# The first half of a threshold attention: four of its slots get their weights turned by TensorE instead of by VectorE and DMA

## The chip, the cores and the metric

The kernel runs on one core of a Trainium2 chip, as one program. The metric is the device time of one launch in microseconds; the kernel before takes 865.78 us, the median of three runs (862.09 to 871.87). Five engines work side by side, each through its own list of instructions in order: TensorE (PE, matrix products), VectorE (DVE), ScalarE (ACT), GpSimd (POOL), and SyncE (SP), which here only issues transfers. A PE product writes to PSUM, a small memory of its own that DVE and ACT read. Transfers are carried out by 16 DMA engines which all queues share. An engine waits at an instruction until the others have signalled that its inputs are ready and its output buffer is free.

## The reference

Two blocks follow one another. First an attention in which only the keys whose score lies within `tau` of the row's largest keep a weight; 8 batches, 8 heads, 576 positions, 64 values a head, all float32:

```
scores = (q @ k.T) / 8
thresh = max(scores, row) - tau
scores = where(scores >= thresh, scores, -1e9)
attn   = exp(scores - max);  attn /= sum(attn) + 1e-9
x      = (attn @ v), heads side by side      # 4608 tokens x 512
h      = x @ w_in                            # 1024 wide
solu   = h * softmax(h)
ln     = (solu - mean) / sqrt(var + 1e-6) * g_ln
out    = ln @ w_out                          # 4608 x 512
```

`w_in` and `w_out` come in as 64-bit floats, and the kernel makes 32-bit ones of them itself.

## The kernel before

**Slots and rounds.** Heads go in pairs. A slot is 128 query rows of the two heads of a pair against all 576 keys; 18 slots make a batch, 144 the whole. Slots 0 to 7 are the first 256 positions of the four pairs of batch 0, two slots to a pair. The main loop goes in rounds, `rnd`; round n does for slot n: the scores (`scores`, L472), the row maxes (`maxes`, L494, DVE), the threshold (`ramp`, L509, ACT, one for each head) and the exponentials with their sums (`exps`, L518, ACT). For slot n-1 it does the division by the sums (`normalise`, L525 to L528, POOL) and `blocks`: DVE transposes the weights in squares of 32 (L540), and after the second slot of a pair three DMAs (L549, L551) move the squares into place, so that keys lie on the partitions (`wT<-T`). Three or four rounds after a pair's second slot the product with v (`attend_steps`, L582, tile `pv`) runs on PE, and ACT copies it (L614) into `xh`, the tokens for the second block.

**The second block, in quarters.** Tokens go in tiles of 128. A tile takes four PE steps, at most one a round: two for h (`ff_h`, L647, against `w_in`) and two for the output (`ff_o`, L752, against `w_out`). Between them lie max, exponential, product, statistics, two normalised copies (`ff_max` L662, `ff_exp` L671, `ff_mul` L677, `ff_stats` L692 and POOL's L696 to L703, `ff_norm` L713, `ff_norm2` L718), four DMAs (`V<-u`, L729) and a transpose (`ff_turn`, L739, tile `uT`). The first two tiles of h need slots 0 to 7, and all of `w_in`; with the kernel before their four quarters stand in rounds 11 to 14.

**The weights.** They come in 16 pieces of 512 KB, one a round: `weight_load` (L270) four rounds ahead, `weight_a` (L284, L287 on DVE, L290 on ACT), `weight_b` (L302, DVE), `weight_c` (L312, POOL), and for `w_out` `weight_gain` (L317, ACT) and a pair of DMAs that lay down a copy with its halves swapped (`w<-w`, L324). The first o step is therefore in round 17 at the soonest.

**Order.** All is issued in the order in which the Python code runs, one list for each engine. What stands around the change: `load_at` says in which round q, k and v of later pairs are loaded (SP's list); `preps` says when those are turned (by `turn`, L337); `pv_due` when a product with v is due; `ready` from which round a tile's h may start; `late`, `middle` and `begin` hold jobs for later rounds. PSUM has two tiles for scores (`s0`, `s1`) and two for all else (`p0`, `p1`, lent by `take` and given back to `pairs_free`).

Of the kernel before, what the change touches and what calls it, by code (L numbers as in the profile page):

```python
# [8 lines left out]
F32 = mybir.dt.float32  # L9
# [7 lines left out]
P = 128  # L17
# [3 lines left out]
def kernel(  # L21
# [47 lines left out]
    ident = const.tile([P, P], F32, name="ident")  # L69
    swapped = const.tile([P, 64], F32, name="swapped")  # L70
    w1 = const.tile([P, NP, DFF], F32, name="w1")
# [24 lines left out]
    xh = {}  # L96
# [5 lines left out]
    def take(name):  # L102
        tag = pairs_free.pop(0)
        return tag, ps_mm.tile([P, 1024], F32, tag=tag, name=name)
# [114 lines left out]
    def constants():  # L219

        nc.gpsimd.memset(seed, 0.0)
        nc.scalar.activation(out=ntau, in_=seed, func=AF.Exp)
        make_identity(nc, ident)
        for g in range(2):
            of = 64 + 32 * (1 - g)
            nc.gpsimd.tensor_copy(
                out=swapped[ROWS[1], 32 * g : 32 * g + 32], in_=ident[ROWS[1], of : of + 32]
            )
        nc.gpsimd.memset(mhalf, -0.5)
        nc.gpsimd.memset(mone, -1.0)  # L230
        nc.gpsimd.memset(zero, 0.0)

        nc.vector.tensor_scalar(
            out=scl, in0=tau_t, scalar1=0.0, scalar2=SCALE, op0=ALU.is_ge, op1=ALU.mult
        )
        nc.vector.tensor_scalar(
            out=tau_t, in0=tau_t, scalar1=0.0, scalar2=104.0, op0=ALU.max, op1=ALU.min
        )  # L240
        nc.vector.tensor_scalar(out=ntau, in0=tau_t, scalar1=-1.0, scalar2=None, op0=ALU.mult)
# [89 lines left out]
    def turn(spare, x, lhsT_of, swap=False):  # L331

        o = spare["base"] + 64 * x
        to = slice(o, o + 64)
        for r in range(2):
            for y in range(2):
                nc.tensor.matmul(  # L337
                    out=spare[r][ROWS[y], to], lhsT=lhsT_of(r, y),
                    rhs=swapped[ROWS[1]] if swap and r else ident[ROWS[r], ROWS[r]],
                    start=True, stop=True,  # L340
                )
# [106 lines left out]
    live = {}  # L448

    def scores(s, items):  # L450
        b, kind, hp, r = slots[s]
# [55 lines left out]
    def ramp(s, x):  # L507
        d = live[s]
        nc.scalar.activation(  # L509
            out=d["w"][x], in_=d["w"][x] if d["loose"] else d["ps"][x][:, 0:S], func=AF.Prelu, bias=d["nth"][x], scale=-1.0,  # L510
            alpha=1.0e30,
        )
# [9 lines left out]
    def normalise(s):  # L522
        d = live[s]
        sm = d["sm"]
        nc.gpsimd.tensor_scalar(out=sm, in0=sm, scalar1=1e-9, scalar2=None, op0=ALU.add)  # L525
        nc.gpsimd.tensor_tensor(out=sm, in0=sm, in1=mone, op=ALU.pow)  # L526
        for x, w in enumerate(d["w"]):
            nc.gpsimd.tensor_scalar(  # L528
                out=w, in0=w, scalar1=sm[:, x : x + 1], scalar2=1.0, op0=ALU.mult, op1=ALU.mult
            )  # L530
# [27 lines left out]


    def attend_steps(key):  # L560
        b, kind, hp = key
        unit = units[key]
        wT = unit["wT"]
        unit["y"] = take("pv")
        _, y = unit["y"]
        y = y.rearrange("p (u n) -> p u n", u=2)

        for e in range(2) if kind == 2 else [None]:
            for m in range(NK):
                for u in range(2):  # L570
                    d, h0 = source(b * NP + (hp if e is None else e + 2 * u))
                    for h in range(2):
                        if e is None:
                            how = "p (r g x) -> p g r x" if b < 2 else "p (g r x) -> p g r x"
                            to = y[ROWS[h], u, 0:P].rearrange(how, r=2, g=2)
                            rhs = wT[ROWS[u], :, m, :, h]
                        else:
                            to = y[ROWS[h], u, 64 * e : 64 * e + 64].rearrange(
                                "p (g x) -> p g x", g=2
                            )  # L580
                            rhs = wT[ROWS[u], :, m, e, h]
# [9 lines left out]
                        yield  # L591

    def attended(key):
        b, kind, hp = key
        tag, y = units.pop(key)["y"]
        y = y.rearrange("p (u n) -> p u n", u=2)[:, :, 0:P]
# [10 lines left out]
        else:  # L607
            if hp == 0:
                xh[b, kind] = work.tile(
                    [P, NP, 256], F32, tag=f"xh{(2 * b + kind) % 4}", bufs=1, name="xh"  # L610
                )
            how = "p (r u y) -> p u r y" if b < 2 else "p (u g x r) -> p u g r x"
# [185 lines left out]
    for s, (b, kind, hp, r) in enumerate(slots):  # L798
        if r == 1:
            pv_due.append((s + LAG_PV + (s < 6 or s in (11, PER - 1, PER + 9)), (b, kind, hp)))  # L800
# [17 lines left out]
    for at, job, hf, what in (  # L818
        (11, load_one, 0, "q"),
        (10, load_one, 0, "k"),  # L820
        (15, load_one, 1, "k"),
        (16, load_one, 1, "q"),
        (17, load_v, 0, (0,)),
        (18, load_v, 0, (1, 2)),
        (PER + 6, load_v, 1, (0,)),
        (PER + 7, load_v, 1, (1, 2)),
    ):
        load_at.setdefault(at, []).append(lambda job=job, hf=hf, what=what: job(1, hf, what))
# [31 lines left out]
    with tc.manual_schedule():  # L860
# [16 lines left out]
        whole = {0: 1, 2: 2, 4: 3}  # L877
        for r, hf, parts in ((0, 0, (0,)), (1, 0, (1, 2)), (3, 1, (0,)), (5, 1, (1, 2))):
            load_at[r] = [lambda hf=hf, parts=parts: load_v(0, hf, parts)]

# [9 lines left out]
        while True:  # L890
# [10 lines left out]
            if rnd == NS:  # L901
# [8 lines left out]
                assert quarter != 3  # L910
            if rnd == 13:
                prev, cur, quarter = cur, None, 0
# [9 lines left out]
            if more:  # L922
# [18 lines left out]
                maxes(rnd, loose)  # L941
                ramp(rnd, 0)
                if rnd == 0:
                    weight_a(0)
                if not loose:
                    keeps(rnd, 0)
                    keeps(rnd, 1)
                ramp(rnd, 1)
                exps(rnd)
            if rnd in whole:  # L950
# [30 lines left out]
            elif step == ("h", 1):  # L981
                ff_h(cur, 1, None, beside)
                quarter = 2
                by = rnd + 2 * (rnd == 14)
                late.setdefault(by, []).append(lambda t=cur: (ff_max(t), ff_exp(t)))
# [9 lines left out]
                if cur == (0, 1, 1):  # L995
                    middle.setdefault(rnd + 6, []).append(lambda t=cur, at=rnd + 6: ff_turn(t, at))
                else:
                    late.setdefault(at, []).append(lambda t=cur, at=at: ff_turn(t, at))
                if not more:
# [15 lines left out]
            if attending is not None:  # L1015
# [6 lines left out]
                elif kind < 2 and hp == NP - 1:  # L1022
                    ready.append((rnd + 1, [(b, kind, 0), (b, kind, 1)]))
            if rnd - 1 in live:
                blocks(rnd - 1)
# [8 lines left out]
            if rnd == 3:  # L1034
                gains()
            if rnd in pieces:
                x = pieces[rnd]
                weight_b(x)
                for y in {0: (3, 4), 11: (), 12: (15,)}.get(x, (x + 4,)):
                    if y < len(pieces):  # L1040
                        weight_load(y)
                if x + 1 < len(pieces):
                    weight_a(x + 1)
            for job in load_at.pop(rnd, []):
# [39 lines left out]
```

## Time and profile before

| | |
|---|---|
| median of three runs | 865.78 us |
| the profiled execution | 864.95 us, of which 863.2 are from the first to the last instruction (the span) |
| TensorE busy | 817.0 us (95%) |
| VectorE, ScalarE, GpSimd busy | 673.5, 572.1, 495.1 us |
| granted TensorE clock, mean | 0.981 of full speed |
| DMA moved | 168.54 MB, 195 GB/s |
| scores of round 6, 9, 11, 13 begin | 39.07, 50.89, 68.22, 79.53 us |
| scores of round 17, 19, 20 begin | 102.52, 116.31, 120.75 us |

The busy share is the time in which an engine has any instruction running; products on PE overlap, so a busy PE is not one at its peak. A wait belongs to the engine that stands idle, and names the one whose signal ended it. The chain that ended last is followed backwards from the last instruction; a line in it is time that the end depended on. A float32 product appears in the trace as two records, each with a weight load of its own (`PEld`). `64*64` is the part of PE's 128 x 128 array that a record uses: four products in different quarters run at the same time.

### The profile page before, as it was taken

To read this page: it belongs to the slowest core of one execution; us is meant where nothing else is said; L and a number is where in the kernel's file an instruction comes from. 1 tells how busy PE (TensorE), PEld (TensorE's weight loads), DVE (VectorE), ACT (ScalarE), POOL (GpSimd) and SP (SyncE) were. 2 spreads that over 40 slices of the span, in tenths; PEclk is the share of its full clock that TensorE was granted. 3 is DMA by queue.
4 is the path that set the end of the run, shared out by engine and by line. 5 is a ranking of instruction groups with operands and counts; after the bars stand their busy time and mean duration, and the time that the engine had idled before them with its cause. 6 is when DMAs were issued, how large, how long until landed. Compare 5 with 4: busy or idle time off the path is not lost.

```text
span 863.2 us, 36114 instructions
## 1 busy us (share of the span) xinstructions
PE 817.0 (95%) x15361; PEld 634.7 (74%) x15361; DVE 673.5 (78%) x1232; ACT 572.1 (66%) x1153; POOL 495.1 (57%) x936
## 2 busy tenths in 40 slices
PE   4659789999999999999999999999999999999997
PEld 3437567777688888888788886777788888887655
DVE  4987777978788888888788887888888888787361
ACT  5876867777667767777677766767677776775121
POOL 2876756566666656565656655565666655555120
PEclk9878999999999999999999999999999999999999
DMA  9999796997878778888788787888788887555312
GB/s 288 243 254 251 185 203 162 234 248 196 224 196 219 202 196 208 220 214 198 201 202 222 198 194 192 212 222 206 183 228 229 193 196 186 154 141 140 69 38 62
DMA packets 83712, 168.54 MB, mean 195 GB/s; under 512 B 15448, under 2 KB 45152, under 8 KB 83552
## 3 DMA queue, kind: packets, MB, share of 16 engines
q1 hardware_dynamic: 82416, 164.25, 75.5%
q8 instruction: 120, 1.97, 1.0%
q10 hardware_dynamic: 1136, 2.00, 0.7%
q14 instruction: 40, 0.33, 0.1%
HBM read 46.14 MB, written 9.44 MB: 64 GB/s over the span
## 4 chain that ended last, share of the span: by engine, by line
PE 84%; DMA 6%; ACT 4%; issue 2%; DVE 2%; POOL 1%; SPq 1%; ACTq 0%; DVEq 0%
PE o_ps L752 26%; PE h_ps L647 23%; PE s_ps L472 16%; PE pv L582 15%; DMA wT<-T 4%; PE h_ps L637 3%; ACT w L509 1%; ACT w L518 1%; DMA qT<-flip 1%; DMA w<-w 1%; DVE w L494 1%; DMA k<-in_k_dram 1%; ACT qT L374 0%; PE s_ps L337 0%; POOL w L528 0%
## 5 line engine op out<-in xcount | busy, mean ns | idle before, releaser
L752 PE MATMUL o_ps<-w,uT 64*64 64x256 f32 x4608 | 273.1, 376 | 4.3 <-issue 1.9
L494 DVE CUSTOM_DVE_ANT_0 w<-s_ps,tau_t 128x576 f32<-128x576 f32 x280 | 200.0, 751 | 94.4 <-PE s_ps L472 67.0
L509 ACT ACTIVATE w<-s_ps,nth 128x576 f32<-128x576 f32 x280 | 197.0, 739 | 110.8 <-DVE nth L494 90.8
L752 PEld LDWEIGHTS o_ps<-w,uT 64*64 64x64 f32 x4608 | 221.5, 133 | 59.3 <-ACT xh L614 12.0
L528 POOL TENSOR_SCALAR w<-w,sm 128x576 f32<-128x576 f32 x288 | 221.5, 781 | 14.3
L540 DVE STREAM_TRANSPOSE T<-w 128x576 f32<-128x576 f32 x288 | 207.5, 755 | 22.0 <-POOL w L528 20.6
L647 PE MATMUL h_ps<-w,xh 64*64 64x512 f32 x1856 | 223.1, 589 | 0.7 <-issue 0.7
L518 ACT ACTIVATE w<-w,ntau 128x576 f32<-128x576 f32 x288 | 219.8, 768 | 0.0
L582 PEld LDWEIGHTS pv<-wT,v 64*64 64x64 f32 x5760 | 179.7, 137 | 37.4 <-issue 12.8
L472 PE MATMUL s_ps<-kT,qT 64*64 64x512 f32 (+1 forms) x2048 | 177.1, 413 | 14.0 <-ACT w L509 12.0
L582 PE MATMUL pv<-wT,v 64*64 64x128 f32 (+1 forms) x5760 | 179.5, 266 | 9.7 <-DMA wT<-T 7.2
L647 PEld LDWEIGHTS h_ps<-w,xh 64*64 64x64 f32 x1856 | 131.7, 133 | 65.4 <-issue 10.6
L525 POOL TENSOR_SCALAR sm<-sm 128x2 f32<-128x2 f32 x144 | 34.7, 241 | 203.7 <-ACT w L518 200.1
L526 POOL TENSOR_TENSOR sm<-sm,mone 128x2 f32<-128x2 f32 x144 | 105.8, 735 | 12.0
L472 PEld LDWEIGHTS s_ps<-kT,qT 64*64 64x64 f32 x2048 | 76.0, 136 | 21.1 <-ACT w L509 16.4
L614 ACT COPY xh<-pv 128x256 f32<-128x256 f32 x64 | 25.0, 390 | 83.3 <-PE pv L582 83.2
L713 ACT ACTIVATE V<-u,nb,rs 128x1024 f32<-128x1024 f32 x36 | 44.7, 1241 | 39.6 <-POOL nb L703 32.6
L739 DVE STREAM_TRANSPOSE uT<-V 128x1024 f32<-128x1024 f32 x36 | 44.3, 1230 | 15.2 <-DMA V<-u 14.8
L518 ACT ACTIVATION_READ_ACCUMULATOR w<-w,ntau 128x1 f32 x288 | 55.9, 194 | 0.0
L677 DVE TENSOR_TENSOR u<-h_ps,u 128x1024 f32<-128x1024 f32 x36 | 42.8, 1189 | 9.7 <-ACT u L671 9.7
L718 DVE TENSOR_SCALAR u<-u,rs,nb 128x1024 f32<-128x1024 f32 x36 | 35.5, 987 | 17.2 <-ACT V L713 17.1
L662 DVE TENSOR_REDUCE hm<-h_ps 128x1 f32<-128x1024 f32 x36 | 43.0, 1193 | 6.0 <-PE h_ps L647 3.3
(88 smaller groups left out, 562.9 us busy)
## 6 DMA issues: line engine op xcount, KB each, us to landing
wT<-T SPq DMA_DIRECT2D x160, 288.0 KB, 6.2
wT<-T SPq DMA_DIRECT2D x64, 576.0 KB, 5.5
V<-u SPq DMA_DIRECT2D x144, 64.0 KB, 3.4
out_dram<-ob SPq DMA_DIRECT2D x71, 128.0 KB, 2.5
q<-in_q_dram SPq DMA_DIRECT2D x24, 288.0 KB, 6.1
qT<-flip SPq DMA_DIRECT2D x48, 144.0 KB, 3.8
k<-in_k_dram SPq DMA_DIRECT2D x24, 288.0 KB, 5.9
kT<-flip SPq DMA_DIRECT2D x48, 144.0 KB, 4.2
```

The source lines that it names most:

```text
L472: nc.tensor.matmul(out=ps[h][ROWS[y], ks], lhsT=lhsT, rhs=d["kT"][ROWS[h], ks], start=True, stop=True,)
L494: nc.vector.tensor_tensor_reduce(out=w, in0=ps[:, 0:S], in1=(zero if loose else tau_t).to_broadcast([P, S]), scale=1.0, scalar=BIG, op0=AL ...
L509: nc.scalar.activation(out=d["w"][x], in_=d["w"][x] if d["loose"] else d["ps"][x][:, 0:S], func=AF.Prelu, bias=d["nth"][x], scale=-1.0, al ...
L518: nc.scalar.activation(out=w, in_=w, func=AF.Exp, bias=ntau, scale=1.0, accum_out=sm[:, x : x + 1])
L526: nc.gpsimd.tensor_tensor(out=sm, in0=sm, in1=mone, op=ALU.pow)
L528: nc.gpsimd.tensor_scalar(out=w, in0=w, scalar1=sm[:, x : x + 1], scalar2=1.0, op0=ALU.mult, op1=ALU.mult)
L540: nc.vector.transpose(out=T[:, :, r, h, :], in_=w)
L582: nc.tensor.matmul(out=to, lhsT=d["v"][ROWS[u], (h0 + h - u) % 4 if b > 1 else h0 + h, m ^ 4 * u if m < 8 and b < 2 else m,], rhs=rhs, sta ...
L647: mm = nc.tensor.matmul(out=h[ROWS[y], f], lhsT=x[ROWS[r], c, ROWS[y]], rhs=w1_parts[ROWS[r], c, part ^ r], start=part == 0 and c == 0, st ...
L713: nc.scalar.activation(out=V, in_=u, func=AF.Identity, bias=nb, scale=rs)
L739: nc.vector.transpose(out=uT, in_=d["V"].rearrange("p y (m x) -> p m y x", x=32))
L752: nc.tensor.matmul(out=d["o"][ROWS[z], 512 * (r ^ other) : 512 * (r ^ other) + 256], lhsT=d["uT"][ROWS[r], m].rearrange("p y x -> p (y x)" ...
```

## The change

For slots 4 to 7 (`EARLY`) the weights are no longer divided by their sums on POOL, transposed on DVE and moved by DMA. Instead

- `ramp` writes the weights so that the keys of one later product are 64 neighbouring columns;
- `normalise` makes a 128 x 128 matrix for each head, `diag`: a permutation (`order`, the old `swapped` with the other half of the columns) times the reciprocal sums;
- `turn_weights`, one round after the slot, multiplies the weights with it on PE, 64 keys a matmul, 18 matmuls a slot, into two PSUM tiles that are held from round 5 to round 9; DVE copies the result to `wT` in three pieces;
- `attend_early`, two rounds after the slot, does the product with v for this one slot, 18 matmuls; ACT copies it to `xh` between the two ramps of that round.

The products of slots 0-1 and 2-3 go into the same two PSUM tiles, in rounds 5 and 7 as before, right after the second ramp; their copies come ahead of that round's exponentials. The first two tiles' h stand in rounds 9 to 12 (from 11 to 14), their later steps two rounds sooner with them, but `ff_turn` of the first not before round 16. The second half of v of batch 0 is loaded in rounds 1 and 2 (from 3 and 5); q, k and v of batch 1 in rounds 6 to 9, 11 and 12 (from 10, 11, 15, 16, 17, 18).

```diff
+    EARLY = range(4, 8)
+    front, turned_w = {}, {}
 def ramp(s, x):
+        to, of = d["w"][x], d["w"][x] if d["loose"] else d["ps"][x][:, 0:S]
+        if s in EARLY:
+            to = to.rearrange("p (m k c) -> p c m k", c=2, m=NK)
+            of = of.rearrange("p (c m k) -> p c m k", c=2, m=NK)
 def normalise(s):
+        if s in EARLY:
+            d["diag"] = diag = work.tile([P, 2, P], F32, tag="uV"[s % 2], bufs=1, name="diag")
+            for x in range(2):
+                nc.gpsimd.tensor_scalar(
+                    out=diag[:, x], in0=order, scalar1=sm[:, x : x + 1], scalar2=1.0,
+                    op0=ALU.mult, op1=ALU.mult,
+                )
+            return
+    def turn_weights(s):
+        d = live.pop(s)
+        pt = front["tiles"]
+        for m in range(NK):
+            of = P * (m % 4) if m < 8 else 512
+            for h, w in enumerate(d["w"]):
+                nc.tensor.matmul(
+                    out=pt[m // 4 % 2][ROWS[h], of : of + P],
+                    lhsT=w[:, 64 * m : 64 * m + 64], rhs=d["diag"][:, h],
+                    start=True, stop=True,
+                )
+        turned_w[s] = wT = work.tile([P, NK, P], F32, tag="wT", bufs=2, name="wT")
+        to = wT.rearrange("p m y -> p (m y)")
+        for of, n, ps in ((0, 512, pt[0]), (512, 512, pt[1]), (1024, P, pt[0][:, 512:])):
+            nc.vector.tensor_copy(out=to[:, of : of + n], in_=ps[:, 0:n])
+    def attend_early(s):
+        b, kind, hp, r = slots[s]
+        wT = turned_w.pop(s)
+        y = front["tiles"][1][:, 512:640]
+        d, h0 = source(b * NP + hp)
+        for m in range(NK):
+            for h in range(2):
+                nc.tensor.matmul(
+                    out=y[ROWS[h]],
+                    lhsT=d["v"][ROWS[h], h0 + h, m ^ 4 * h if m < 8 else m],
+                    rhs=wT[ROWS[h], m], start=m == 0, stop=m == NK - 1,
+                )
+        nc.scalar.copy(out=xh[b, kind][:, hp, P * r : P * r + P], in_=y)
...
-        (11, load_one, 0, "q"),
-        (10, load_one, 0, "k"),
-        (15, load_one, 1, "k"),
-        (16, load_one, 1, "q"),
-        (17, load_v, 0, (0,)),
-        (18, load_v, 0, (1, 2)),
+        (7, load_one, 0, "q"),
+        (6, load_one, 0, "k"),
+        (8, load_one, 1, "k"),
+        (9, load_one, 1, "q"),
+        (11, load_v, 0, (0,)),
+        (12, load_v, 0, (1, 2)),
...
+            if rnd == EARLY[0] + 1:
+                front["tags"], front["tiles"] = zip(take("pt"), take("pt"))
-            if rnd == 13:
+            if rnd == 11:
                 prev, cur, quarter = cur, None, 0
...
                 ramp(rnd, 0)
+                if rnd - 2 in EARLY:
+                    attend_early(rnd - 2)
...
+                    if rnd - 2 == EARLY[-2]:
+                        ready.append((rnd + 1, [(0, 0, 0), (0, 0, 1)]))
                 ramp(rnd, 1)
+                if "tiles" in front and pv_due[0][0] <= rnd:
+                    key = pv_due.pop(0)[1]
+                    for _ in attend_steps(key):
+                        pass
+                    attended(key)
                 exps(rnd)
...
-                by = rnd + 2 * (rnd == 14)
+                by = rnd + 2 * (rnd == 12)
...
-            if rnd - 1 in live:
+            if rnd - 1 in EARLY:
+                weights_on(rnd)
+                turn_weights(rnd - 1)
+            elif rnd - 1 in live:
                 blocks(rnd - 1)
```

`weights_on` is the old passage that steps the weight pieces on, made a function; in rounds 5 to 8 it is called ahead of the turn.

## The prediction

> **What bounds the kernel now.** I read the page first: TensorE (PE) works 817.0 of 863.2 us. That is a mean, so I then asked for PE's waits after 120 us and got six entries, 1.9 + 1.9 + 0.9 + 0.7 + 0.4 + 0.4 = 6.2 us in 743 us. From there on PE is the bound, and nothing outside PE's own sum matters. Before 120 us it waits. So I next read busy time by stretch, one stretch per round from round 9 to round 13 and from 17 to 19 (columns: from:to and length, then busy us of PE, weight loads, VectorE (DVE), ScalarE (ACT), GpSimd (POOL), then granted PE clock, DMA share, GB/s):
>
> ```profile
> 50.89:59.03 8.14, 6.10 (x86) 4.30 (x90) 6.93 (x14) 5.64 (x12) 6.88 (x10) 0.58 1.02 276
> 59.03:68.22 9.19, 5.53 (x94) 4.28 (x94) 4.04 (x9) 4.49 (x9) 6.18 (x8) 0.69 1.03 257
> 68.22:73.16 4.94, 4.94 (x58) 3.33 (x56) 3.11 (x7) 3.86 (x8) 0.00 (x0) 0.89 0.99 243
> 73.16:79.53 6.37, 6.37 (x122) 4.81 (x118) 5.35 (x11) 4.73 (x10) 4.96 (x9) 1.00 1.13 243
> ...
> 102.52:109.01 6.49, 5.02 (x80) 3.00 (x84) 5.93 (x10) 6.49 (x16) 3.21 (x6) 1.00 0.81 198
> 109.01:116.31 7.30, 5.50 (x121) 3.52 (x116) 4.93 (x10) 4.06 (x11) 4.96 (x11) 1.00 0.91 206
> ```
>
> Rounds 9 and 10 are the longest, no engine fills them, the clock is granted at 0.58 and 0.69, and the DMA engines are full. The timeline of PE says why (start, length, what, idle before it and its releaser):
>
> ```profile
> 54.49 0.69 PE L582 MATMUL pv<-wT,v 64*64 64x128 f32 x4 [1.32 <-DMA wT<-T]
> 55.55 3.76 PE L582 MATMUL pv<-wT,v 64*64 64x128 f32 x66 [0.37 <-DMA wT<-T]
> ...
> 63.64 0.69 PE L582 MATMUL pv<-wT,v 64*64 64x128 f32 x4 [3.25 <-DMA wT<-T]
> 64.74 3.89 PE L582 MATMUL pv<-wT,v 64*64 64x128 f32 x66 [0.41 <-DMA wT<-T]
> ...
> 69.72 3.80 PE L647 MATMUL h_ps<-w,xh 64*64 64x512 f32 x32
> ```
>
> The products of slots 4-5 and 6-7 wait for the DMAs that turn the weights, and then run at half speed. The first h starts at 69.72. The chain that ended last adds the price of one such transfer, one later wait that will matter, and the tail's blocks over all 128 rows (start, length, what):
>
> ```profile
> 53.37 11.33 DMA wT<-T
> ...
> 108.75 6.19 DMA w<-w
> ...
> 788.85 3.63 PE h_ps L637 x8
> ...
> 800.36 7.06 PE h_ps L637 x16
> ...
> 816.59 13.93 PE h_ps L637 x32
> ```
>
> **What the sum must give.** From round 13 on the PE order of the two kernels is the same, and from round 20 (its scores start at 120.75) PE is full. So the change is worth what it moves the start of round 20 by. I walk there round by round, for after.
>
> **Prices.** PE: 70 records of pv take 1.91 us warm (148.16 in the chain), four quarters at a time, so a 128-column record takes some 0.106 us in its quarter. A *turn* of one slot is 18 matmuls, 36 records, over 128 rows and half the columns, two side by side: 18 x 0.106 = 1.91 us. Whether its weight loads hide is not in any row of this shape. Nearest rows: the tail's blocks take 13.93 - 7.06 = 6.87 us for 16 more records, 0.429 each, against the 0.427 of streaming that 3.41 us for 32 records of h, four at a time, give; so 128-row loads (190 ns each) hide there, and 7.06 - 16 x 0.429 = 0.2 us is left as the cost of a block for changing shape. Low end 1.91; high end 36 loads of 133 ns one after another, 4.8 us. I take 1.91 + 0.2 = 2.1, because the nearest row hides its loads. The *early product* of one slot is 36 records in two quarters, 1.91 us, where a pair of slots took 1.91 before. PE gets 4 x 2.1 + 4 x 1.91 - 2 x 1.91 = 12.2 us more work, all of it in the waiting stretch.
>
> On that 0.2: the Trainium skill, "TensorEngine Tiling (Array Packing)", Key Properties, says that a change of tiling mode drains the engine. The trace's 0.2 us a block agrees; without it each turn would be 1.91 and the result 0.8 us lower.
>
> DVE: 128x256 out of PSUM takes 0.42 (L399), 128x64 0.21, so 512 columns some 0.70 and 128 some 0.28; three copies, each starting some 0.07 us before the one ahead ends, 1.5 us. Low end 0.42 each for 512 (L284, from SBUF), 1.1 in all. They replace two transposes, 1.36 us from start to start. About even. ACT: eight copies of 128x128, some 0.3 each (between 0.25 for 64 columns and 0.39 for 256), for four of 0.39: +0.8 us. The ramp now writes every second element; L399 does so too and takes 0.39 for 256 columns, as the plain L614 does, so nothing (high end: twice, +0.74 each, eight of them). POOL: two 128x128 products for two of 128x576, 0.36 (between 0.24 and 0.78) for 0.78: 0.8 us less a slot, off the path. The third copy that builds `order` (0.2 us near 1.8) is over long before q is turned (6.8). DMA: two units of 576 + 2 x 288 KB go, 2.36 MB; from 40 to 82 the queue moves 254 GB/s at a full share. Into that stretch come k and q of the second half and v, 2.2 MB. Even, and the same transfers then no longer stand in the queue at 98 to 122 us.
>
> **The walk.** Scores are 0.97, an h quarter or an o quarter 3.41.
> - Round 5: the product of slots 0-1 runs 35.65 to 39.3 as now (it waits for ACT's qe). The turn of slot 4 waits for the two copies ACT makes of it (0.5), 39.8 to 41.9; behind it wait the scores of round 6, at 41.9 instead of 39.07. The exps of round 5 are now behind those copies on ACT, 37.4 to 39.85; their first reader is the turn of round 6 at 44.8, so that hides.
> - Round 6: 0.97 + 1.91 + 2.1 = 5.0, round 7 at 46.9. DVE beside it: maxes 1.36, weights 1.3, copies 1.5; the copies wait for the turn, and behind them wait the next maxes, 0.4 us. On ACT the copy of the early product stands between the two ramps and holds the second, and so the next scores, till 45.8; PE is on the turn till 46.9, which covers it (were the turn free, 1 us would show).
> - On SP v of the second half, now in rounds 3 and 5, goes ahead of the wT of round 2 (issued at 23.86): some 1.5 us of issue, and its reader starts at 35.65. Hidden.
> - Round 7: 0.97 + 1.91 + 1.91 + 0.5 (copies of slots 2-3 ahead of the turn) + 2.1 = 7.4; round 8 at 54.3.
> - Round 8: 5.0; round 9 at 59.3. The **first h** at 59.3 + 0.97 + 1.91 = 62.2, that is 7.5 us sooner.
> - Round 9: 6.3; scores 10 at 65.6. Here PE stops being what paces the rounds. DVE per round: maxes 1.36, transposes 1.36, weight pieces 1.25, and one of ff_max 1.15, ff_mul 1.1, stats 1.4, norm2 0.9. From the maxes of round 10 at 66.9 that is 5.1, 5.1, 5.4, 4.9, 5.1, so the maxes of round 15 are at 92.5 (now 92.47). The 7.5 us are **spent again** by then: the two h less in rounds 13 and 14 are time in which PE waits, since o needs the last weight piece, one piece a round. One more: the last piece is loaded behind the wT of round 12 and may land some 1 us late: 93.5.
> - Rounds 15 to 17: now ACT's V waits for POOL's nb in round 15 (92.82); in after it is ff_exp of the second tile that stands there, to about 95. Scores 16 at 98.5 (now 98.1); round 17's o waits for uT, behind maxes, stats, transposes 5.3 us after 99.8: 105.1 (now 105.5). Scores 18 at 108.5 (now 109.0).
> - Round 18: now o waits till 114.98 for the last swap of w2, issued at 107.93 behind ACT's gain at 107.02 and next to 512 KB of q and of v. In after, ff_exp (1.2 us) is not ahead of the gain, and q and v have gone: gain by 105.5, landing 4 to 7 us later, 110.5 to 113.5; o runs 109.5 to 112.9. Scores 19 at 113.4 to 114.5, now 116.31. In round 19 V (1.24) is no longer ahead of the k copies, some 0.7 more.
> Round 20 starts 2.5 to 4 us sooner; I take 3.3. The waits near 170 us (0.93 + 0.65 and a cold product, 3.74 for 2.17) stay, within 2 us. Profiled execution: 864.95 (span 863.2 and 1.75 around it) - 3.3 = 861.7. The median shown is 0.8 above it, so 865.8 - 3.3 = **862.5**.
>
> **Rivals.**
> - *A, slower: the turn's weight loads do not hide.* 4.8 for 2.1 us, four times +2.7 = +10.8, all ahead of the maxes of round 10, from which DVE has no slack: 862.5 + 10.8 = 873.3. It decides from 2.9 us a turn on, where 4 x 0.8 eats the gain. With it the first h is at 73, later than 69.72, and the change doesn't do what it says. For it: loads of 133 ns under streams of 106 ns. Against: the tail's 0.429. Chance 0.2. The Trainium skill speaks for it, "TensorE: Matmul & The Clock Gate", Part 3: a weight load overlaps running matmuls only where its row group differs, and the turn uses all rows. By that rule A holds; the tail's rows, with all rows used too, go against the rule at 427 ns streams, and none shows shorter ones.
> - *B: the loads come at the wrong time.* k, q, ends and v (3.4 MB) now start in rounds 6 to 12, into a full queue, 2.36 MB leave it. The 1.1 MB between, at 254 GB/s, are 4.3 us if weight pieces or the wT of round 10 land that late: 866.8. For it: landings of 9 to 10 us there. Against: a piece has three rounds. Chance 0.15.
> - *C: the head start is carried through.* If PE, not DVE, paced rounds 10 to 18, all 7.5 us would last: 858.3, and 856 with the queue freed. For it: the chain runs on PE from 64.7 to 84.3. Against: the 5.1 us of DVE a round. Chance 0.15.
>
> **The numbers.** Forecast 0.5 (its own range 858.5 to 867), A 0.2, B 0.15, C 0.15. The range takes in most of A and of C: 856 to 873. A measurement here tells about 1% from no change, 857.1 to 874.4. Faster by more: 0.12 (most of C's lower half and a little of the forecast); slower by more: 0.12 (A's upper half); within: 0.76.
>
> **What would show it.** In the profile after: the turns' 36 records in 2.1 us; no wait of PE for wT<-T before 75 us; h from about 62 us; DVE without idle time in rounds 10 to 14; an o of round 18 that hardly waits for w<-w; PE full from about 117 us. I am wrong if the turns take 3 us, if ACT or DVE wait for raw, or if waits after 150 us change by more than 2 us.

## The result and the profile after

The changed kernel takes 871.88 us, the median of 20 runs (867.73 to 879.16), and the kernel before 863.69 us in 20 runs beside them (858.99 to 872.47). The ratio is **1.0099** with a 95% interval of 1.0075 to 1.0123: slower by 8.5 us (6.5 to 10.6). Forecast were 862.5 us and a gain of 3.3, in a range of 856 to 873; the time lies inside the range, the sign is wrong. The profiled execution of after is the slowest of its 20, 879.16 us with a span of 877.4, so a second trace of each kernel was taken: spans 872.3 and, for before, 862.2.

The waits of PE after 120 us, the first view that was read of before, now have five entries (engine, line, releaser: us in total, times, longest):

```profile
PE pv L633 <- DMA wT<-T: 3.7, 3, 3.0
PE s_ps L476 <- issue: 2.9, 2, 2.4
PE o_ps L812 <- issue: 2.3, 2, 2.1
PE pv L633 <- issue: 1.7, 2, 1.1
PE s_ps L338 <- DVE both L498: 0.8, 2, 0.5
```

That is 11.4 us where before had 6.2; "issue" grows from 3.5 to 6.9. PE is still the bound from there on. Busy time by stretch of after, one round per line from round 9 to round 15 and for 17 and 18 (from:to and length; PE, weight loads, DVE, ACT, POOL; PE clock, DMA share, GB/s):

```profile
61.70:68.45 6.75, 6.49 (x87) 4.44 (x89) 5.45 (x12) 4.80 (x12) 3.65 (x5) 1.00 0.48 159
68.45:72.96 4.51, 4.51 (x53) 2.19 (x49) 2.79 (x6) 2.79 (x6) 3.75 (x6) 1.00 0.25 58
72.96:77.75 4.79, 4.64 (x53) 1.92 (x45) 4.49 (x9) 3.87 (x8) 3.84 (x5) 1.00 0.75 179
77.75:84.74 6.99, 6.64 (x119) 4.65 (x123) 6.96 (x15) 6.00 (x12) 5.75 (x10) 1.00 1.04 250
84.74:90.05 5.31, 2.31 (x65) 1.29 (x60) 5.30 (x12) 5.11 (x11) 4.70 (x9) 0.96 0.81 187
90.05:96.21 6.16, 3.42 (x83) 1.60 (x81) 6.16 (x12) 5.08 (x15) 5.03 (x6) 0.76 1.00 231
96.21:106.61 10.40, 6.50 (x150) 5.24 (x146) 5.81 (x11) 6.68 (x15) 4.72 (x7) 0.67 0.85 205
...
111.25:117.66 6.41, 4.98 (x90) 2.96 (x86) 6.02 (x12) 6.41 (x14) 4.02 (x9) 1.00 0.56 131
117.66:122.67 5.01, 5.01 (x120) 3.69 (x116) 3.60 (x7) 3.83 (x11) 2.40 (x4) 1.00 0.68 179
```

The two worst rounds of before, 9 and 10, have lost their waits: full clock, DMA share 0.48 and 0.25. PE fills rounds 9 to 12. Then the place of the loss moves: DVE fills rounds 12 to 14 (18.42 of 18.46 us), PE works 2.31 of 5.31 and 3.42 of 6.16 us in rounds 13 and 14, the clock falls to 0.67, and round 15 takes 10.40 us, against 6.99 before. The timeline of PE in after shows the added work (start, length, what, idle before it and its releaser):

```profile
41.63 1.21 PE L476 MATMUL s_ps<-kT,qT 64*64 64x64 f32 x16
43.14 2.18 PE L600 MATMUL pt<-wT,v 64*64 64x128 f32 x36 [0.30 <-DVE wT L591]
45.25 2.19 PE L583 MATMUL pt<-diag,w 128*64 128x128 f32 x36
47.37 1.21 PE L476 MATMUL s_ps<-kT,qT 64*64 64x64 f32 x16
...
51.37 2.18 PE L633 MATMUL pt<-wT,v 64*64 64x128 f32 x68 [0.15 <-ACT xh L606]
53.83 2.19 PE L583 MATMUL pt<-diag,w 128*64 128x128 f32 x36 [0.27 <-ACT xh L657]
...
64.97 0.64 PE L707 MATMUL h_ps<-w,xh 64*64 64x512 f32 x1
```

A turn is 2.12 us from its start to that of the next scores (45.25 to 47.37); its 36 weight loads of 137 ns, 4.9 us if one followed another, do not show in it. The first h is at 65 us, 4.75 sooner than before. From scores to product it is 1.51 us (41.63 to 43.14) where the prediction had 0.97.

The first maxes of rounds 10, 14 and 15 and the `ff_max` that waits for the early h, in DVE's timeline:

```profile
69.91 0.76 DVE L498 CUSTOM_DVE_ANT_0 w<-s_ps,tau_t 128x576 f32<-128x576 f32 x1 [2.64 <-PE s_ps L476]
...
73.26 1.22 DVE L722 TENSOR_REDUCE hm<-h_ps 128x1 f32<-128x1024 f32 x1 [0.56 <-PE h_ps L707]
...
92.25 0.74 DVE L498 CUSTOM_DVE_ANT_0 w<-s_ps,tau_t 128x576 f32<-128x576 f32 x1
...
98.30 0.76 DVE L498 CUSTOM_DVE_ANT_0 w<-s_ps,tau_t 128x576 f32<-128x576 f32 x1 [0.90 <-PE s_ps L476]
```

Where the time came from (starts of the scores, us, unless named):

| | before | forecast | after | after, second trace |
|---|---|---|---|---|
| round 6 | 39.07 | 41.9 | 41.63 | 41.88 |
| round 7 | 42.03 | 46.9 | 47.37 | 47.62 |
| round 9 | 50.89 | 59.3 | 61.70 | 61.95 |
| first h | 69.72 | 62.2 | 64.97 | 65.22 |
| round 10 | 59.03 | 65.6 | 68.45 | 68.70 |
| first max of round 15 (DVE) | 92.47 | 92.5 | 98.30 | 99.58 |
| round 16 | 98.11 | 98.5 | 106.61 | 106.22 |
| round 18 | 109.01 | 108.5 | 117.66 | 116.28 |
| round 20 | 120.75 | 117.5 | 127.82 | 126.70 |

One relation makes every trace of this study comparable. Span less the start of round 20 less PE's waits behind it is nearly the same in all 17 traces: 734.6 to 739.0 us. So a kernel's time is the start of round 20 plus those waits plus some 737 us, to within 2 to 3 us. First pair of traces: 7.1 later at round 20 and 4.8 more waits (10.6 for 5.8), 14.2 in the span, so 2.3 are in neither; second pair: 7.1 and 3.5, 10.1 in the span.

### The profile page after: what moved, and what is told of

It is laid out like the page before. It is cut to its first block, busy times and chain, and to the rows that moved or that the text cites. A ratio compares the mean times of both kernels' runs of the same rounds, so it can differ in the third digit from the quotient of the medians.

```text
span 877.4 us, 36405 instructions
## 1 busy us (share of the span) xinstructions
PE 830.9 (95%) x15505; PEld 613.5 (70%) x15505; DVE 673.7 (77%) x1236; ACT 573.5 (65%) x1157; POOL 490.9 (56%) x937
## 4 chain that ended last, share of the span: by engine, by line
PE 84%; DMA 5%; ACT 4%; issue 2%; DVE 2%; SPq 2%; POOL 0%; ACTq 0%; DVEq 0%
PE o_ps L812 26%; PE h_ps L707 23%; PE s_ps L476 15%; PE pv L633 14%; PE h_ps L697 3%; DMA wT<-T 2%; DMA v<-in_v_dram 1%; ACT w L517 1%; ACT w L525 1%; PE pt L600 1%; SPq L566 1%; PE pt L583 1%; PE pt L633 1%; DMA V<-u 1%; DVE wT L591 1%
## 5 line engine op out<-in xcount | busy, mean ns | idle before, releaser
L812 PE MATMUL o_ps<-w,uT 64*64 64x256 f32 x4608 | 269.2, 376 | 3.0 <-issue 2.3
L543 POOL TENSOR_SCALAR w<-w,sm 128x576 f32<-128x576 f32 x280 | 215.5, 782 | 13.9
L707 PE MATMUL h_ps<-w,xh 64*64 64x512 f32 x1856 | 219.9, 593 | 0.0
L555 DVE STREAM_TRANSPOSE T<-w 128x576 f32<-128x576 f32 x280 | 201.6, 755 | 20.5 <-POOL w L543 20.5
L633 PEld LDWEIGHTS pv<-wT,v 64*64 64x64 f32 x5472 | 160.7, 136 | 37.0 <-issue 22.1
L476 PE MATMUL s_ps<-kT,qT 64*64 64x64 f32 (+1 forms) x2048 | 172.2, 418 | 10.0 <-ACT w L517 6.1
L707 PEld LDWEIGHTS h_ps<-w,xh 64*64 64x64 f32 x1856 | 110.0, 134 | 87.0 <-issue 69.9
L633 PE MATMUL pv<-wT,v 64*64 64x128 f32 (+1 forms) x5472 | 162.2, 262 | 5.5 <-DMA wT<-T 3.7
L476 PEld LDWEIGHTS s_ps<-kT,qT 64*64 64x64 f32 x2048 | 68.5, 137 | 17.7 <-ACT w L517 8.8
L731 ACT ACTIVATE u<-h_ps,hm 128x1024 f32<-128x1024 f32 x36 | 40.1, 1115 | 12.1 <-DMA V<-u 9.4
```

What stands on the lines that cost most here:

```text
L476: nc.tensor.matmul(out=ps[h][ROWS[y], ks], lhsT=lhsT, rhs=d["kT"][ROWS[h], ks], start=True, stop=True,)
L543: nc.gpsimd.tensor_scalar(out=w, in0=w, scalar1=sm[:, x : x + 1], scalar2=1.0, op0=ALU.mult, op1=ALU.mult)
L555: nc.vector.transpose(out=T[:, :, r, h, :], in_=w)
L633: nc.tensor.matmul(out=to, lhsT=d["v"][ROWS[u], (h0 + h - u) % 4 if b > 1 else h0 + h, m ^ 4 * u if m < 8 and b < 2 else m,], rhs=rhs, sta ...
L707: mm = nc.tensor.matmul(out=h[ROWS[y], f], lhsT=x[ROWS[r], c, ROWS[y]], rhs=w1_parts[ROWS[r], c, part ^ r], start=part == 0 and c == 0, st ...
L812: nc.tensor.matmul(out=d["o"][ROWS[z], 512 * (r ^ other) : 512 * (r ^ other) + 256], lhsT=d["uT"][ROWS[r], m].rearrange("p y x -> p (y x)" ...
```

## The experiments

All ratios are against the kernel before on the same chip; in us they are taken of 863. "Round 20" and "waits" (PE's, behind round 20) are from one trace each, the ratio from 4 to 23 runs a side, so the two columns need not agree to a few us.

| kernel | ratio, 95% interval | us against before | round 20 | waits |
|---|---|---|---|---|
| before | | 0 | 120.8, again 119.6 | 5.8, 5.2 |
| after | 1.0099 (1.0075 to 1.0123) | +8.5 | 127.8, again 126.7 | 10.6, 8.7 |
| e7 turns doubled | 1.0219 (1.0176 to 1.0262) | +18.9 | 135.9 | 6.4 |
| e2 other order of copies | 1.0126 (1.0100 to 1.0152) | +10.9 | 127.1 | 5.4 |
| e1 v of batch 1 back | 1.0064 (1.0039 to 1.0089) | +5.5 | 123.9 | 6.4 |
| e4 loads alone | 1.0049 (1.0030 to 1.0068) | +4.2 | 121.1 | 3.8 |
| e6 turn alone | 1.0098 (1.0066 to 1.0130) | +8.5 | 128.4 | 8.3 |
| e5 turn and early h, old loads | 1.0143 (1.0107 to 1.0179) | +12.3 | 129.1 | 8.4 |
| e3 turn and loads, old h | 1.0042 (1.0019 to 1.0065) | +3.6 | 122.0 | 8.2 |
| e8 two slots, h in 10 | 1.0011 (0.9980 to 1.0042) | +0.9 | 114.3, again 122.1 | 6.6, 5.6 |
| e10 two slots, h in 11 | 0.9999 (0.9970 to 1.0029) | -0.1 | 117.3 | 5.4 |
| e9 two slots, h in 10, old loads | 1.0045 (1.0012 to 1.0078) | +3.9 | 121.1 | 9.6 |
| e14 two slots, h in 10, v back | 0.9984 (0.9954 to 1.0015) | -1.4 | 117.4 | 3.7 |
| e15 two slots, h in 11, v back | 1.0005 (0.9971 to 1.0038) | +0.4 | 117.9 | 7.0 |

### Is PE's work in rounds 5 to 8 paid at the end?

**e7**: each matmul of the turn is issued twice.

```diff
                 nc.tensor.matmul(out=pt[...], lhsT=w[...], rhs=d["diag"][:, h], start=True, stop=True)
+                nc.tensor.matmul(out=pt[...], lhsT=w[...], rhs=d["diag"][:, h], start=True, stop=True)
```

> The changed kernel with each of the turn's matmuls issued twice into the same place: 8.5 us (4 x 2.1) more TensorE work in rounds 5 to 8, nothing else. If these rounds are paced by TensorE and nothing later gives it back (VectorE has no slack from round 10 on): scores of round 10 and of round 20 both 8.5 us later, 880 us. If about half is given back by the old waits in rounds 10 to 14, as it seemed (10.8 late at round 9, 5 late at round 12): 4 us at round 20, 876. If DVE's copies pace the rounds: under 2 us, 873.

880.89 us. In its PE timeline the scores of rounds 6, 7 and 9 start here (41.63, 47.37 and 61.70 in after):

```profile
43.65 1.21 PE L476 MATMUL s_ps<-kT,qT 64*64 64x64 f32 x16
...
51.40 1.21 PE L476 MATMUL s_ps<-kT,qT 64*64 64x64 f32 x16
...
69.72 1.21 PE L476 MATMUL s_ps<-kT,qT 64*64 64x64 f32 x16
```

Later by 2.02, 4.03 and 8.02 us, some 2.0 for each turn so far, and still by 8.1 at round 20; the medians differ by 9.0, and by the ratios it is 10.4, give or take 4.2. **Nothing gives it back.** So in after PE is the bound of rounds 5 to 8, and what is added there is still there at the end. (The one trace of e7 ends only 1.1 and 6.2 us behind the two of after, because it happens to have 4.2 and 2.3 us less of waits behind round 20.) The doubled turn also has the price without its change of shape: 2.0 us for 36 more records, so 0.1 of the 2.12 is the block's own cost.

**e2**: DVE copies the second PSUM tile ahead of the first, in case the order of the copies holds the product up.

```diff
-        for of, n, ps in ((0, 512, pt[0]), (512, 512, pt[1]), (1024, P, pt[0][:, 512:])):
+        for of, n, ps in ((512, 512, pt[1]), (0, 512, pt[0]), (1024, P, pt[0][:, 512:])):
```

> The changed kernel with the copy of the second PSUM tile made ahead of that of the first, since the early product, which writes into the second tile, was seen to start only after that copy (43.14, with the copies from 41.79). Theory 1: the 0.3 us in which PE waits ahead of each of the four early products goes, and no more, since PE work fills the rest of the loop: round 9 starts 1 to 1.3 us sooner, time 1 us lower. Rival (the loop is paced by VectorE's copies, not by PE): 0.65 us a round, round 9 some 2.6 us sooner.

Round 9 starts at 61.23 instead of 61.70, 0.47 us sooner where 1 to 1.3 were expected, and the time is not lower (873.01). The order of the copies is not what costs.

### The wait in round 14

In after's ACT timeline one wait stands out, and the list of SP's queue says what is ahead of it (start and length of the issue):

```profile
100.62 1.11 ACT L731 ACTIVATE u<-h_ps,hm 128x1024 f32<-128x1024 f32 x1 [3.72 <-DMA V<-u]
```

```profile
89.20 0.95 SPq L271 DMA_DIRECT2D raw<-in_moe_w_out_dram  x1
90.20 1.83 SPq L176 DMA_DIRECT2D v<-in_v_dram  x2
92.08 1.27 SPq L181 DMA_DIRECT2D v<-in_v_dram  x2
93.45 1.20 SPq L325 DMA_DIRECT2D w<-w  x2
94.74 4.42 SPq L789 DMA_DIRECT2D V<-u  x4
```

`ff_exp` of the second tile needs the buffer `u`, from which the four `V<-u` of the first are still read. Their issue comes behind v of batch 1, at 94.74, and takes 4.42 us. The chain that ended last goes through the same transfers:

```profile
91.41 6.92 DMA v<-in_v_dram
98.34 2.20 DMA V<-u
```

**e1** puts v of batch 1 back to rounds 17 and 18.

```diff
-        (11, load_v, 0, (0,)),
-        (12, load_v, 0, (1, 2)),
+        (17, load_v, 0, (0,)),
+        (18, load_v, 0, (1, 2)),
```

> The changed kernel with v of batch 1 loaded in rounds 17 and 18 again; all else as changed. Theory 1 (two losses: the PE loop of rounds 5 to 8, and in round 14 ScalarE's ff_exp standing 3.7 us till the four V<-u transfers, queued behind v, have read the only u buffer): the 3.7 us wait falls under 1 us, round 16 starts some 3.5 us sooner after round 15, round 20 starts at about 124.5 instead of 127.8, time 3 us below the changed kernel, 4 to 5 above the kernel before. Rival (V<-u is late by itself, v is not the cause): the wait stays over 3 us and the time does not move.

868.18 us; by the ratios 3.0 less than after, give or take 3.0. e2 ran on the same chip as e1, has v early like after, and its `ff_exp` has a wait of 3.94 us: its six runs (870.22 to 875.58) all lie above those of e1 (864.25 to 869.88), by 4.8 in the median. SP's queue and ACT in e1:

```profile
92.32 2.49 SPq L789 DMA_DIRECT2D V<-u  x4
```

```profile
98.12 1.11 ACT L731 ACTIVATE u<-h_ps,hm 128x1024 f32<-128x1024 f32 x1
```

`V<-u` goes out 2.4 us sooner and in 2.49 us, `ff_exp` waits for nothing, round 15 takes 6.3 us for 10.4, and round 20 starts 4.0 sooner (2.9 sooner than in after's second trace). That trace has the same wait, 2.81 us, so it belongs to the change. Whether v costs by its place in the queue or by its share of the DMA engines is not taken apart here. It isn't v alone: e5 below, with v late and the rest of the old loads, has 2.15 us of it (`V<-u` then lands at the end of a chain with `wT<-T`), and e3, with h in its old rounds and v early, has none.

### Turn, early h and loads taken apart

**e4** is the kernel before with the new load rounds alone; **e3** the changed kernel with the first h in rounds 11 to 14; **e5** the changed kernel with q, k and v of batch 1 in the old rounds; **e6** has e3's and e5's edits, so that the turning and the early products are left.

```diff
 e3, e6:
-                        ready.append((rnd + 1, [(0, 0, 0), (0, 0, 1)]))
+                        ready.append((rnd + 3, [(0, 0, 0), (0, 0, 1)]))
-            if rnd == 11:
+            if rnd == 13:
-                by = rnd + 2 * (rnd == 12)
+                by = rnd + 2 * (rnd == 14)
 e5, e6:
-        (7, load_one, 0, "q"), (6, load_one, 0, "k"), (8, load_one, 1, "k"), (9, load_one, 1, "q"),
-        (11, load_v, 0, (0,)), (12, load_v, 0, (1, 2)),
+        (11, load_one, 0, "q"), (10, load_one, 0, "k"), (15, load_one, 1, "k"), (16, load_one, 1, "q"),
+        (17, load_v, 0, (0,)), (18, load_v, 0, (1, 2)),
```

> The kernel before with nothing changed but the loads in front: second half of v of batch 0 in rounds 1 and 2, q, k and v of batch 1 in rounds 6 to 9, 11 and 12. Theory 1 says the loads cost only where V<-u stands behind v: here V<-u of the first tile is in round 15, so no such wait; but the weight transfers of slots 4 to 7 stand in a fuller queue: 0 to 3 us slower than before, round 11 later by as much, round 18's wait for w<-w shorter. Rival (earlier loads are the loss): 6 us or more slower. Rival (they are the gain, and the turning eats it): 3 us or more faster.

> The changed kernel with the first h in rounds 11 to 14 as in the kernel before; the turning by TensorE, the early products and the loads as changed. Theory 1 (the loss is in rounds 5 to 8 and in the wait of ff_exp, the earlier h gains a little in itself): rounds 9 to 13 run 2 h quarters shorter, rounds 13 to 15 longer, the wait of ff_exp for V<-u goes, round 20 at 124 to 127, time 0 to 3 us below the changed kernel, so still above the kernel before. Rival (the earlier h is what costs): time equal to the kernel before or below it. Rival (the earlier h is a gain that the rest eats): time 5 us or more above the changed kernel.

> The changed kernel with q, k and v of batch 1 loaded in the old rounds (10, 11, 15 to 18); turn and first h as changed, v of batch 0 still early. Theory L (the early loads have a price of their own: v in round 12 stands ahead of V<-u in the queue, q and k stand in the full queue of rounds 6 to 9): the 3.7 us wait of ff_exp goes as in the run with v put back, the scores of round 20 come 3.9 us or more sooner than in the changed kernel, and with k and q gone too the time is 864 to 866, below the 868.2 of the run with v put back. Rival (only v mattered; k and q early are free, because no turn by DMA is left to be held up): 868, as with v put back. Second rival (old loads bring back the old waits of round 18 and 19): 870 to 872.

> The changed kernel with the old load rounds and with the first h in rounds 11 to 14 as before: what is left is the turning by TensorE and the early products. Theory T (the extra TensorE work of rounds 5 to 8 is itself paid in part at the end): the scores of round 10 still start some 4 us later than before, those of round 20 1 us or more later, and the time is 864 to 866. Rival (turning by itself is even, the early loads make the rest): 862 +- 1, no difference from before, and scores of round 20 within 0.5 us of it. A gain (860 or less) would say that the turn is worth having and that loads and early h spoil it.

| | old loads | new loads |
|---|---|---|
| old turn, old h | 0 | e4 +4.2 |
| turn by PE, old h | e6 +8.5 | e3 +3.6 |
| turn by PE, early h | e5 +12.3 | after +8.5 |

The table is not wholly square: e5 and e6 keep the early v of batch 0, which the kernel before does not have. The parts do not add up, and the expectations were missed: e5 and e6 came out above every number that was expected of them, e4 at 4.2 for 0 to 3, and e3 gained 4.9 on after where 0 to 3 were expected.

- **The turn** costs 8.5 us with the old loads and nothing that can be told from zero (3.6 for 4.2, each give or take 2) with the new ones.
- **The loads** cost 4.2 us in the kernel before and win 4.9 and 3.8 beside the turn (both give or take some 3.5). Two lines suggest why; they do not show all of it. In e4 the transfers that turn the weights are still there, and by its PE timeline its product of slots 6-7 waits twice as long as the 3.25 of before. But that trace is of a run of 863.09 us, where e4's median is 866.57, with round 20 at 121.1 and 3.8 us of waits, so the loss itself is not in it:

```profile
66.84 4.67 PE L582 MATMUL pv<-wT,v 64*64 64x128 f32 x70 [6.95 <-DMA wT<-T]
```

In e5, where the loads are late, q goes out at 114.35, right ahead of the last swap of `w_out` at 115.49, and o of round 18 waits for that swap (2.2 us in e6; none in after and e3), about half of what the early loads win; the two traces of before have it at 1.80 and 4.04:

```profile
122.14 0.87 PE L812 MATMUL o_ps<-w,uT 64*64 64x256 f32 x10 [2.62 <-DMA w<-w]
```

- **Early h** costs 3.8 us (e5 less e6) and 4.9 (after less e3; the first alone would not be clear of zero). From round 9 to round 20 it is 66.1 us in after and 61.7 in e3: 1.9 of the 4.5 lie in rounds 9 to 14, 2.6 in round 15 with `ff_exp`'s wait. In after h stands in rounds 9 and 10, and round 9 is the longer for it (6.75 us for e3's 3.29; round 10 4.51 for 4.68), and it is missing in rounds 13 and 14, where DVE sets the pace and PE has room (2.31 of 5.31 us in round 13).

### Half the turn, and the search for a better kernel

**e8** turns slots 6 and 7 alone, with h in rounds 10 to 13; **e10** has h in 11 to 14; **e9** is e8 with the old loads of batch 1; **e14** and **e15** are e8 and e10 with v of batch 1 back in 17 and 18.

```diff
 e8:
-    EARLY = range(4, 8)
+    EARLY = range(6, 8)
-                        ready.append((rnd + 1, [(0, 0, 0), (0, 0, 1)]))
+                        ready.append((rnd + 2, [(0, 0, 0), (0, 0, 1)]))
-            if rnd == 11:
+            if rnd == 12:
-                by = rnd + 2 * (rnd == 12)
+                by = rnd + 2 * (rnd == 13)
```

> The changed kernel with only slots 6 and 7 turned by TensorE (slots 4 and 5 again by VectorE and DMA), first h in round 10, loads as changed. Half of the extra TensorE work is gone. Theory W (the extra work of rounds 5 to 8 sets how late round 10 is): scores of round 9 some 4 to 5 us later than before rather than 10.8, first h at about 60 to 62, scores of round 20 at 122 to 125 (ff_exp of the second tile still waits for V<-u behind v, +3), 866 to 868. Rival (the product of slots 4 and 5 waits for its DMA as before, and the loss only changes its name): scores of round 10 as late as in the changed kernel, 871.

> The changed kernel with two slots turned by TensorE (6 and 7) and the first h in rounds 11 to 14 as before. Early h has cost 4.9 and 5.6 us with four slots turned (two pairs of runs). Theory H (an h in rounds 9 and 10 is paid because TensorE sets the pace there, and TensorE waits instead in rounds 13 and 14): late h wins here too, by less since only round 10 is moved, 1 to 4 us: 859 to 862, the fastest of all. Rival (early h is bad only where the turns have already made TensorE late): no change from 863, or a loss of up to 3, since the head start of 6.5 us in the profile with two slots comes from the early h.

> Two slots turned by TensorE, first h in round 10, and q, k and v of batch 1 in the old rounds. With four slots turned the early loads have won 3.4 and 4.1 us (a wait of o for w<-w at round 18 goes); with none they lost 4.4 (the turns by DMA wait in the full queue). Theory (the gain of the early loads is the w<-w wait, 2.2 to 2.6 us, and the loss is the DMA turn that stays): here one of two DMA turns in that stretch is left, so the two nearly cancel: 862 to 865. Rival (the early loads win as long as h is early): 866 to 868.

> Two slots turned, first h in round 10, v of batch 1 again in rounds 17 and 18; q and k stay early. If v in rounds 11 and 12 costs wherever it stands (it fills the queue ahead of V<-u and the last weight pieces): 860 to 861, some 2 to 3 below the 863.1 with v early. If it cost only because ff_exp of the second tile came right behind it (in the trace of two slots ff_exp waits for nothing over 0.6 us): no change, 863, or up to 2 worse, because v then stands in the queue at 98 to 110 us beside the last swap of w2, which o of round 18 waits for.

> Two slots turned, first h in rounds 11 to 14 as before, v of batch 1 again in rounds 17 and 18. As for the kernel with h in round 10: 860 to 861 if v early costs wherever it stands, 863 to 865 if it costs only behind an early h and otherwise frees the queue for the last swap of w2.

With half the turn the loss is gone: e8, e10, e14 and e15 are all within 1.4 us of before, with intervals that hold 1. That is better than the 866 to 868 expected of e8, and e10 is not the fastest of all that it was expected to be: late h, worth 4.9 with four slots, is worth nothing that shows here; with the old loads (e9, 867.02) the loss is 3.9 again, as the rival of that run had it. e14 has the lowest median of all, 861.55, and can't be told from before. **No version that beats both was found.**

### Second traces

> Two slots turned, first h in round 10, a second trace of that kernel. If its gain at round 20 is real and given back later: scores of round 20 at 113 to 116, and again an issue wait of 3 to 4 us near 217 to 220, with other waits after it. If the first trace was luck: scores of round 20 at 118 to 121, a front with waits of TensorE for wT<-T or w<-w of 3 us or more, and a time of 863 or above.

> The kernel before once more, for a second trace. If one trace is good for the walk: scores of round 20 start within 1 us of 120.8 and the waits of the products for wT<-T in rounds 9 and 10 are within 1 us of 1.3 and 3.3. If the full queue makes them differ from run to run: several us apart, with the difference in those waits, and then differences of one trace below that say nothing.

> The changed kernel once more, for a second trace. The loss of rounds 5 to 8 (scores of round 9 10.8 us later than before) is TensorE's work and must be there within 0.7 us. The wait of ff_exp for V<-u in round 14 (3.7 us) hangs on the queue: 2 to 5 us if it is part of the change's cost, 0 to 1 if it was chance. Scores of round 20 at 125 to 128; its first trace was of the slowest of 20 runs, so a time nearer to the median, 870 to 873, with fewer or shorter waits after 120 us.

The first trace of e8 had round 20 at 114.3, 6.5 us ahead of before, which looked like a gain that the median lost again. The second has it at 122.1. Of the 7.8 us between them, 3.4 are there at round 9, behind a wait of 3.11 us for `wT<-T` in round 7 (0.56 in the first). Then the product in round 16 waits again; the first line is from the first trace, the second from the second:

```profile
97.37 0.44 PE L633 MATMUL pv<-wT,v 64*64 64x128 f32 x4 [1.76 <-DMA wT<-T]
...
104.43 0.58 PE L633 MATMUL pv<-wT,v 64*64 64x128 f32 x4 [4.83 <-DMA wT<-T]
```

So that head start belongs to one run and not to the kernel. The two traces of before differ in the same way: its product of slots 6-7 waits 3.25 + 0.41 us in one and 1.27 + 0.83 in the other (round 15 then 2.9 sooner), and the w<-w wait of 4.04 takes most of that back by round 20. In these pairs single waits for a transfer differ by 2 to 3 us, and the start of a round by up to 7.8; a walk from one trace is no better than that. After's rounds 5 to 10, which PE fills, repeat within 0.3 us.

## Why the prediction was wrong

The frame held: time is the start of round 20 plus PE's waits behind it. The start was forecast 3.3 us sooner, at 117.5, and came at 127.82, 10.3 us off: 2.85 by round 10, another 2.95 by the first max of round 15, 2.3 in round 15 and 2.2 from there to round 20. The waits behind it, put down as unchanged "within 2 us", grew by 4.8 and 3.5. No single step makes the loss. In the order of the steps:

1. **Prices of the pieces: right.** Turn 2.12 us (2.1 forecast), the three DVE copies 1.49 (1.5), an ACT copy 0.27 (0.3). So rival A, the weight loads that don't hide, is out: 36 records over 128 rows stream at 0.11 us in each half with their loads of 137 ns beside them. The rule of the Trainium skill, "TensorE: Matmul & The Clock Gate", Part 3, that a load overlaps only where the row group differs, would have made it 4.8; this trace goes against it also for short streams. A's time, 873.3, came nearest to the result by luck: its mechanism did not act.
2. **Rounds 5 to 8: 2.4 us short at round 9, 2.85 at round 10.** This step failed by what it put at nothing: the sum 0.97 + 1.91 + 2.1 left out the hand-overs between engines. The product waits for DVE's copies and starts 1.51 us after the scores (+0.54 a round), takes 2.11 and not 1.91 (+0.2), and in round 7 ACT's two copies between three users of one PSUM tile make 3.20 of 2.41. e7 shows that time added here reaches the end.
3. **Rounds 10 to 15: right engine, wrong pace, another 2.8 us.** (PE's order is the same in both kernels from round 15 on and not from 13, as I wrote: before has h in 13 and 14.) DVE paces rounds 12 to 14, as forecast, but the maxes are 6.26, 5.10, 5.33, 5.65 and 6.05 us apart and not 5.1, 5.1, 5.4, 4.9, 5.1; in the first of these DVE waits 0.56 for the early h. The head start was forecast to be "spent again" at no loss; e3 shows early h as a cost of 4.9 us (e5 less e6 has 3.8, not clear of zero).
4. **Rounds 15 to 17: the step that failed outright.** I put `ff_exp` of the second tile "to about 95" and scores 16 at 98.5. It ran at 100.62, held 3.72 us by `V<-u` behind v in SP's queue; scores 16 came at 106.6, 8.1 late, of which 5.8 were there at the first max of round 15. The v that I had leave the queue at 98 to 122 us I did not follow to where it arrived, at 90. With v put back, in e1, round 20 starts 2.9 to 4.0 us sooner and the time is 3.0 lower, give or take 3.0.
5. **Round 18: right.** o does not wait for `w<-w` any more, and round 18 takes 5.01 us for 7.30; e5 and e6 bring the wait back. This gain is there and too small: from round 16 to round 20 after needs 21.2 us where the forecast had 19.0, with o of round 17 behind a late transpose (0.67) and 5.15 us in round 19 for a forecast of 3.6.
6. **After round 20: wrong.** The "issue" waits grew by 3.4 and 4.9 us (6.9 and 7.4 for 3.5 and 2.5); those for wT<-T by 1.8 and -0.4. By the prediction's own sign (waits after 150 us that change by more than 2 us) it was wrong here too. The "issue" waits are longer with four turned slots: 4.4 to 7.4 us in the eight traces of such kernels, 1.6 to 3.5 in the three without the turn, 1.0 to 6.6 in the six with two slots; why is not shown.

Rival B (loads at the wrong time, 866.8) was right in one place, v ahead of `V<-u`, and wrong as a sum: beside the turn the new loads win 3.8 to 4.9. Rival C, the head start carried through, is out. The 0.12 for slower stood for a time over 1% above before, and the result, 0.99% above, lies at the edge of the band that had 0.76. But most of that chance was A's, whose mechanism did not act. The range of the walk came from bounds on prices: hand-overs had none, and queue positions only B's, which counted bytes and not places in the queue.

What stays open: why the turn is free beside the new loads and costs 8.5 without them (the w<-w and `ends` waits in e6 make some 4.5 of it by its one trace, and the rest isn't placed; that trace is of a run of 877.03 us, where e6's median is 870.39), and why the "issue" waits are longer with the turn.

## What to carry to other kernels

Work added to the engine that is the bound is paid in full where that engine has no wait left in the same rounds (e7), so count the idle time that the added work really meets, hand-over by hand-over, ahead of pricing the work itself. A transfer that is moved forward must be followed to the small transfers that it then stands in front of in its queue. And parts of one change can hang on one another: here the loads lose alone and win beside the turn, so that undoing one part of a change tells its worth only in the company of the others.

## What was not expected of the hardware

PE's "issue" waits, with no semaphore behind them, mostly come back at the same instruction in each trace of one kernel. Here are those of over 1.5 us behind 120 us in the two traces of before and of after (PE timelines):

```profile
136.41 2.96 PE L752 MATMUL o_ps<-w,uT 64*64 64x256 f32 x49 [1.89 <-issue]
```

```profile
135.02 2.96 PE L752 MATMUL o_ps<-w,uT 64*64 64x256 f32 x49 [1.62 <-issue]
```

```profile
248.25 1.30 PE L812 MATMUL o_ps<-w,uT 64*64 64x256 f32 x19 [2.10 <-issue]
...
436.94 1.48 PE L476 MATMUL s_ps<-kT,qT 64*64 64x64 f32 x16 [2.41 <-issue]
```

```profile
242.90 1.50 PE L812 MATMUL o_ps<-w,uT 64*64 64x256 f32 x19 [2.37 <-issue]
...
433.62 1.21 PE L476 MATMUL s_ps<-kT,qT 64*64 64x64 f32 x16 [2.59 <-issue]
```

These three differ by 0.2 to 0.3 us between two runs; others differ more (0.94 and 2.09 us in round 15 of before, 3.64 and 1.17 in two traces of e8, near 220 and 228 us). They sit in other places in other kernels: 1.0 to 7.4 us a trace behind round 20 over the study. The page lists an own DMA queue for instructions, in after:

```profile
q8 instruction: 122, 2.00, 1.0%
```

122 packets of 16 KB, some 7 us apart. All 33 of PE's "issue" waits of 0.9 us or more in the 17 traces (behind the first 20 us) stand in the same place to such a packet: it begins 2.3 to 3.1 us and ends 1.2 to 1.7 us ahead of the wait's end. So these are instructions that come late, as far as traces without an experiment can show it. That full DMA engines delay them is not shown: the packets ahead of eleven of these waits took 0.9 to 1.4 us, as most packets do (median 1.1).
